# First token group's outputs stored and added in later passes, gating iterations moved into the first pass, weight sums reordered, first step in its own product order

## The chip, the cores and the metric

The kernel runs on one core of one Trainium2 chip. The metric is device time in microseconds (us). TensorE (PE) multiplies matrices into banks of the accumulation memory (PSUM); VectorE (DVE) and ScalarE (ACT) read those banks and write to on-chip memory; SyncE (SP) issues the transfers between on-chip memory and device memory, in one queue in order. Before the change the median of three runs was 1779.27 us (1777.72 to 1779.35).

## The reference

`q`, `k`, `v`, `a_re`, `a_im` have the shape (4, 8, 768, 48); `x` has 3072 tokens of 384 numbers; there are 8 experts with 1024 hidden units.

```python
for t in range(S):                                   # linear attention with a complex decay
    new_re = ar * S_re - ai * S_im
    new_im = ar * S_im + ai * S_re
    S_re, S_im = new_re + k[t] v[t]^T, new_im
    y[t] = q[t] @ S_re
x = y.transpose(0, 2, 1, 3).reshape(3072, 384)

logits = x @ w_gate                                  # 384 -> 8
P = np.exp(logits - logits.max())
for _ in range(8):                                   # the gating iterations
    P /= P.sum(1, keepdims=True) + 1e-09             # rows
    P /= P.sum(0, keepdims=True) + 1e-09             # columns
    P *= N / E
out = 0
for e in range(E):
    out += P[:, e:e + 1] * (np.maximum(x @ w1[e], 0) @ w2[e])
```

The gates P are needed only where an expert's output is added to the sum, since every expert runs on every token.

## The kernel before, in words

**Phase 1** (up to about 601 us of the profiled span) runs the attention in 12 blocks of 256 tokens and sends experts 0 and 1 along with it, block by block: `experts()` puts the first layer into `ph` (L183 to L185), the second into `po` (L162 to L164) and stores the result through `yst` to `ye_d[0]` and `ye_d[1]` in device memory. The attention's result goes as a high and a low part to `x_d`.

**Phase 2a** (L766, about 601 to 642 us) runs experts 0 and 1 for the last block. Beside it DVE and ACT build what phase 2b multiplies for the first group of 768 tokens: `load_x` (L612) loads six blocks of x (`whole`: a high part into `xt`, a low part into one of three `low` buffers, and their sum, L635), makes the sums of blocks (`form`, L645 and L647) and splits them into a high part (ACT) and a low part (`lower`, L653). `whole_w` (L745) prepares the weights of one step. `check` (L560) tests the data's range and ends with a transposition of its verdict on PE (`okp`, L573); `sinkhorn` (L577) takes the exponential; then come `HEAD` = 3 gating iterations, `rows` on DVE (L596) and `columns` (L604), whose column sum is a small matrix product with ones on PE (`cp`, L606).

**Phase 2b** (L800) runs experts 2 to 7 in 4 passes (one per group of 768 tokens) of 16 steps each, numbered n = 0 to 63. A step covers three slices of 128 hidden units of an expert and forms the first layer from 15 products instead of 18 (a fast matrix multiplication of 3x3 by 3x2 blocks): each product is a sum of weight blocks times a sum of x blocks, and takes three matmuls of 384 columns (high times high, high times low, low times high: L937, L938, L939). Two PSUM banks, A and B, are read out in turn: ACT copies the first product of a chain (L950), DVE adds or subtracts the others into `s` (L953, L972, L975), ACT applies the relu and rounds to the high part (L957), DVE takes the low part (L964). After each product come one or two of the 18 pieces of the second layer of the step before (L866 to L868), so a step is 99 matmuls. The list `slots[m]` holds side work that DVE, ACT and SP do after product m.

In the first pass (n < 16) that side work is above all the weights of step n + 1: 13 sums of weight blocks on DVE (`sums`, L714), their high parts on ACT (`hi`, L722), low parts on DVE (`lo`, L731), and stores to `w_d`, from which `fetch_w` (L764) loads them in the later passes. The raw weights come in two transfers (`raw_w`, L683). The weights of a step fill four buffers, a to d, out of a ring of `WIDE` = 11. Steps 1 to 5 of the first pass also run the last five gating iterations, with `rows` after product 6 and the column sum at the step's end; step 6 multiplies the six tiles gathered so far by their gate (L899). A finished tile of 128 tokens leaves its bank through `evict` (L832): ACT with the gate as scale for the first of the experts (L837, L839), DVE with a multiply and add for the others (L841). `mixin` (L827) adds experts 0 and 1 from `ye_d`. From step 4 or 6 on each pass also builds the x forms of the next group, one job at a time (`deal`).

What sets the order: PE's instructions run in the order of the program all through. In phase 2b DVE and ACT do so too (L1013). In phases 1 and 2a DVE and ACT, and everywhere SP, are ordered by the compiler's planner, which estimates when each instruction can run.

Of the kernel before, what the change touches and what calls it, by code (L numbers as in the profile page):

```python
# [6 lines left out]
F32 = mybir.dt.float32  # L7
F32R = mybir.dt.float32r
U8 = mybir.dt.uint8
AF = mybir.ActivationFunctionType  # L10
# [15 lines left out]
WIDE = 11  # L26
# [12 lines left out]
HEAD = 3  # L39
# [19 lines left out]
class Net:  # L59
# [9 lines left out]
    def build(self):  # L69
# [3 lines left out]
        with ExitStack() as ctx:  # L73
# [35 lines left out]
            self.ye_d = [[dram.tile([128, C], F32, name=f"ye_d{u}_{i}") for i in range(self.ntt)] for u in range(2)]  # L109
# [450 lines left out]
    def check(self, sp, more=lambda k: None):  # L560
        nc, ok, fl, ns = self.nc, self.ok, self.fl, self.N // SUB
        P = self.P.rearrange("p t e -> p (t e)")
        t = sp.tile([128, max(P.shape[1], fl.shape[1])], F32, name="chk")
        for j, (src, thr, op) in enumerate((
                (fl[:, 0:ns], 2.0 ** 40, ALU.is_le), (fl[:, ns:2 * ns], 2.0 ** 18, ALU.is_le),
                (fl[:, 2 * ns:-2], 1e-24, ALU.is_ge), (fl[:, -2:-1], 2.0 ** 40, ALU.is_le), (fl[:, -1:], 2.0 ** 18, ALU.is_le), (P, 3e38, ALU.is_le), (P, -3e38, ALU.is_ge))):
            o = t[:, :src.shape[1]]
            nc.vector.tensor_scalar(o, src, thr, None, op)
            nc.vector.tensor_reduce(ok[:, j:j + 1], o, AX.X, ALU.min)
        nc.vector.tensor_reduce(ok[:, 7:8], ok[:, 0:7], AX.X, ALU.min)  # L570
        more(2)
        tp = self.psK.tile([1, 128], F32, tag="po", name="okp")
        nc.tensor.transpose(tp, ok[:, 7:8], self.ident)  # L573
        nc.vector.tensor_reduce(ok[0:1, 8:9], tp, AX.X, ALU.min)
        nc.vector.tensor_copy(self.oki, ok[0:1, 8:9])

# [35 lines left out]
    def load_x(self, u, avail, temp, low):  # L612
# [43 lines left out]
        def plain(n, c, j):  # L656
# [9 lines left out]
            whole(*x11), whole(*x12), whole(*x21), whole(*x22),  # L666
            form(8, x11, x12, ADD), form(12, x21, 8, SUB), lower(8), form(9, x22, 12, ADD), lower(12), lower(9),
# [24 lines left out]
    def prep_w(self):  # L692
# [34 lines left out]
        def lo(q):  # L727
            t, k, src = parts[q]

            def run():  # L730
# [3 lines left out]
                if q == 3:  # L734
# [462 lines left out]
```

## Time and profile before

| | us |
|---|---|
| median of three runs | 1779.27 |
| the profiled execution | 1779.32 |
| its span | 1777.6 |
| phase 2a, in the span | 600.7 to 641.8 |
| first pass (16 steps) | 641.9 to 934.1 |
| passes 2 to 4 (48 steps) and the end | 934.1 to 1777.6 |

Some 1.7 us of the profiled execution lie around its span. In the rows of the profile `L12` is line 12 of the kernel; a group of instructions reads as count | busy us, mean ns of one | idle us of the engine just before them, and what ended it. A row of windows gives the busy time of each engine in a stretch, with the instruction count in brackets, then the share of TensorE's full clock that was granted, the share of the transfer engines and GB/s. A transfer's row ends in its size and the microseconds from issue to landing.

### The profile page before, as it was taken

What the parts mean: (1) busy time and instruction counts of PE and PEld (TensorE: products, weight loads), DVE (VectorE), ACT (ScalarE), POOL (GpSimd) and SP (SyncE); (2) the same over time, 40 slices, a digit from 0 to 9 for tenths busy, and PEclk for the clock granted to TensorE, in tenths of its full rate; (3) what the DMA queues carried; (4) which work ended last, traced back from release to release, by engine and by line L of the source; (5) the groups of instructions that cost most, each with busy time, mean ns of one, the idle gap of its engine ahead of it and who ended that gap; (6) DMA issues with size and microseconds to landing.
All of it is one profiled execution on the core that took longest, in us unless ns stands there. A gap on an engine that the chain in (4) does not pass through costs nothing.

```text
span 1777.6 us, 30741 instructions
## 1 busy us (share of the span) xinstructions
PE 1719.3 (97%) x11736; PEld 1677.5 (94%) x11736; DVE 1303.0 (73%) x2940; ACT 749.5 (42%) x1663; POOL 6.4 (0%) x15
## 2 busy tenths in 40 slices
PE   5889999999999889999999999999999999999998
PEld 3889999999999879999999999999999999999998
DVE  7888999999993669989995556655466765546564
ACT  7544554554543444544543433333433333333332
POOL 1000000000000000000000000000000000000000
PEclk9899999999999999999999999999999999999999
DMA  6333343333343657667787556667565657555560
GB/s 216 96 111 119 115 121 123 120 98 119 114 103 103 205 189 253 224 237 268 246 309 263 186 184 206 219 232 229 196 199 177 224 194 249 174 187 188 201 207 29
DMA packets 170044, 321.62 MB, mean 181 GB/s; under 512 B 13984, under 2 KB 129440, under 8 KB 169888
## 3 DMA queue, kind: packets, MB, share of 16 engines
q1 hardware_dynamic: 169088, 319.17, 54.3%
q8 instruction: 95, 1.56, 0.4%
q14 instruction: 61, 0.50, 0.1%
q10 hardware_dynamic: 800, 0.39, 0.1%
HBM read 226.64 MB, written 73.92 MB: 169 GB/s over the span
## 4 chain that ended last, share of the span: by engine, by line


## 5 line engine op out<-in xcount | busy, mean ns | idle before, releaser
L957 ACT ACTIVATE hh<-s 128x384 fp32r<-128x384 f32 x384 | 201.7, 526 | 447.1 <-DVE s L953 400.2
L953 DVE TENSOR_TENSOR s<-s,A 128x384 f32<-128x384 f32 x316 | 174.5, 552 | 141.9 <-PE A L939 140.6
L866 PE MATMUL po<-w_d,hh 128*128 128x384 f32 x768 | 257.2, 335 | 0.0
L868 PE MATMUL po<-w_d,hl 128*128 128x384 f32 x768 | 257.2, 335 | 0.0
L867 PE MATMUL po<-w_d,hh 128*128 128x384 f32 x768 | 257.2, 335 | 0.0
L964 DVE SCALAR_TENSOR_TENSOR hl<-s,hh 128x384 fp32r<-128x384 f32 x384 | 212.1, 552 | 6.9
L189 ACT ACTIVATE hh<-ph 128x256 fp32r<-128x256 f32 x192 | 73.4, 382 | 232.0 <-PE ph L185 231.4
L184 PE MATMUL ph<-xl,w 128*128 128x256 f32 x576 | 163.3, 283 | 3.4 <-DVE xl L536 3.3
L185 PE MATMUL ph<-xh,w 128*128 128x256 f32 x576 | 162.9, 283 | 0.0
L183 PE MATMUL ph<-xh,w 128*128 128x256 f32 x576 | 162.5, 282 | 0.1
L866 PEld LDWEIGHTS po<-w_d,hh 128*128 128x128 f32 x768 | 144.4, 188 | 0.5 <-DVE oa L841 0.3
L868 PEld LDWEIGHTS po<-w_d,hl 128*128 128x128 f32 x768 | 144.5, 188 | 0.0
L867 PEld LDWEIGHTS po<-w_d,hh 128*128 128x128 f32 x768 | 144.3, 188 | 0.0
L953 DVE TENSOR_TENSOR s<-s,B 128x384 f32<-128x384 f32 x192 | 106.0, 552 | 51.6 <-PE B L939 48.8
L950 ACT ACTIVATE s<-B 128x384 f32<-128x384 f32 x192 | 93.6, 487 | 109.8 <-PE B L939 107.6
L162 PE MATMUL po<-w,hh 128*128 128x384 f32 x384 | 137.4, 358 | 1.3 <-ACT yst L167 1.3
L972 DVE TENSOR_TENSOR s<-s,B 128x384 f32<-128x384 f32 x64 | 35.4, 553 | 129.7 <-PE B L939 129.5
L163 PE MATMUL po<-w,hh 128*128 128x384 f32 x384 | 130.0, 338 | 0.0
L164 PE MATMUL po<-w,hl 128*128 128x384 f32 x384 | 129.8, 338 | 0.0
L868 PE MATMUL po<-w_c,hl 128*128 128x384 f32 x384 | 128.4, 334 | 0.0
L866 PE MATMUL po<-w_c,hh 128*128 128x384 f32 x384 | 128.3, 334 | 0.0
L867 PE MATMUL po<-w_c,hh 128*128 128x384 f32 x384 | 128.3, 334 | 0.0
(235 smaller groups left out, 4079.9 us busy)
## 6 DMA issues: line engine op xcount, KB each, us to landing
w_d<-w_d SPq DMA_DIRECT2D x64, 768.0 KB, 6.3
w_a<-w_d SPq DMA_DIRECT2D x48, 768.0 KB, 7.6
w_b<-w_d SPq DMA_DIRECT2D x48, 768.0 KB, 4.2
w_c<-w_d SPq DMA_DIRECT2D x48, 768.0 KB, 4.4
raw<-in_w_dram SPq DMA_DIRECT2D x32, 576.0 KB, 5.2
w_d<-w_a SPq DMA_DIRECT2D x16, 768.0 KB, 3.2
w_d<-w_b SPq DMA_DIRECT2D x16, 768.0 KB, 4.4
w_d<-w_c SPq DMA_DIRECT2D x16, 768.0 KB, 5.9
```

What stands on the lines that cost most here:

```text
L162: nc.tensor.matmul(po[k], hh[:, s], w2h, start=f == 0, stop=False)
L163: nc.tensor.matmul(po[k], hh[:, s], w2l, start=False, stop=False)
L164: nc.tensor.matmul(po[k], hl[:, s], w2h, start=False, stop=f == NF - 1)
L183: nc.tensor.matmul(ph, w[:, 0, cs], xh[:, ct, :], start=(ct == 0), stop=False)
L184: nc.tensor.matmul(ph, w[:, 0, cs], xl[:, ct, :], start=False, stop=False)
L185: nc.tensor.matmul(ph, w[:, 1, cs], xh[:, ct, :], start=False, stop=(ct == NCT - 1))
L866: nc.tensor.matmul(po[k], hh[:, s], w2[:, 0], start=c == 0, stop=False)
L867: nc.tensor.matmul(po[k], hh[:, s], w2[:, 1], start=False, stop=False)
L868: nc.tensor.matmul(po[k], hl[:, s], w2[:, 0], start=False, stop=c == NF - 1)
L953: V.tensor_tensor(S[nm], S[nm], ps, op)
L957: A.activation(hh, S[nm], AF.Relu)
L964: V.scalar_tensor_tensor(hl, S[nm], 0.0, hh.bitcast(F32), ALU.max, ALU.subtract)
```

## The change

1. **Outputs of the first group.** In pass 1 `evict` no longer weights and adds: ACT copies each finished tile out and SP stores it to `ye_d`, which now exists for all eight experts for the first six tiles. In passes 2 to 4 each step loads one such tile (`late`) and adds it with its gate (`join`), 6 tiles by 8 experts in 48 steps. The new buffers `mo` and `my` come out of the ring of weight buffers, which shrinks from 11 to 10.
2. **Gating.** `check`, `sinkhorn` and the three iterations leave phase 2a. A generator, `gating`, does the range test, the exponential and all eight iterations in steps 1 to 14, at most six small portions per step, and asks for a PSUM bank at a step's end when it needs PE.
3. **Weights.** Phase 2a prepares the weights of steps 0 and 1, so step 0 prepares none. The sums come in another order and earlier slots, and the high and low parts in other slots (the prefix `hi(0)` moves from slot 2 to slot 3).
4. **First step.** Step 0 has no second layer to interleave. It now takes its products in the order `FIRST`, with the B chain in two banks: four products in B, copied once to `sb` and added from there, and four in F.
5. **x forms.** `load_x` loads and sums in another order; the forms for the second group are dealt from step 5 on, after products 6 and 12.

```diff
-WIDE = 11
+WIDE = 10
-WOPS = [2, 1, 7, 11, 3, 8, 12, 13, 4, 6, 14, 10, 0, 9, 5]
+WOPS = [2, 8, 6, 1, 12, 14, 3, 4, 7, 13, 10, 11, 0, 9, 5]
 PRODS = [("B", 3), ("A", 8), ("B", 12), ("A", 13), ("B", 7), ("C", 9), ("B", 1), ("C", 5), ("B", 11), ("D", 2), ("B", 10), ("E", 14), ("B", 4), ("E", 0), ("B", 6)]
+FIRST = [("B", 3), ("A", 8), ("C", 9), ("B", 12), ("A", 13), ("E", 14), ("B", 7), ("C", 5), ("B", 1), ("F", 11), ("D", 2), ("E", 0), ("F", 10), ("F", 4), ("F", 6)]
...
-            whole(*x11), whole(*x12), whole(*x21), whole(*x22),
-            form(8, x11, x12, ADD), form(12, x21, 8, SUB), lower(8), form(9, x22, 12, ADD), lower(12), lower(9),
...
+            whole(*x11), whole(*x21), form(3, x11, x21, SUB), whole(*x12), form(8, x11, x12, ADD), lower(3),
+            form(12, x21, 8, SUB), lower(8), whole(*x22), form(9, x22, 12, ADD), lower(12), lower(9),
+            whole(*x31), form(1, x12, x31, SUB), form(2, x11, x31, ADD), lower(1), lower(2), whole(*x32), form(5, x12, x32, ADD), lower(5),
...
+    def gating(self):
...
+        V.tensor_reduce(mx, flat, AX.X, ALU.max)
+        g = yield from bank([1, 128])
+        nc.tensor.transpose(g, mx, self.ident)
...
+        V.tensor_scalar(P, P, gm, None, ALU.subtract)
+        nc.scalar.activation(P, P, AF.Exp)
+        yield
+        for k in range(ITERS):
+            V.tensor_reduce(rs, P, AX.X, ALU.add)
+            yield
+            V.tensor_scalar(rs, rs, 1e-9, None, ALU.add)
+            V.reciprocal(rs, rs)
+            yield
+            V.tensor_tensor(P, P, rs.unsqueeze(2).broadcast_to([128, self.ntt, E]), ALU.mult)
+            yield
+            V.tensor_reduce(cs, P.rearrange("p t e -> p e t"), AX.X, ALU.add)
+            g = yield from bank([128, E])
+            nc.tensor.matmul(g, self.ones, cs, start=True, stop=True)
+            V.tensor_scalar(cs, g, 1e-9, None, ALU.add)
+            yield
...
-        more(1)
-        self.check(xa, more)
-        self.sinkhorn(xa, more)
-        for k in range(HEAD):
-            self.rows()
-            more(3)
-            self.columns(self.psK.tile([128, E], F32, tag="po", name=f"cp{k}"))
-            if k == 1:
-                self.raw_w(0)
-                self.raw_w(1)
-                self.whole_w()
+        for _ in range(2):
+            self.raw_w(0)
+            self.raw_w(1)
+            self.whole_w()
...
+        def late(m, q):
+            tt = tile_of(0, m)
+            t = home[q] = self.xa.tile([128, C], F32, tag="my" if q else "mo", name=f"m{q}_{tt}", bufs=2)
+            nc.sync.dma_start(t, self.ye_d[q][tt])
+
+        def join(m, q):
...
+                V.scalar_tensor_tensor(o, home[q], self.P[:, tt, q:q + 1], o, ALU.mult, ALU.add)
...
         def evict(u, e, k):
+            if u == 0:
+                st = self.xa.tile([128, C], F32, tag=f"oa{k}", name=f"st{e}_{tt}")
+                A.activation(st, po[k], AF.Copy)
+                nc.sync.dma_start(self.ye_d[e][tt], st)
+                return
...
-            if n + 1 < NT:
+            if 1 <= n and n + 1 < NT:
                 slots[1] += [sums(0, 3)]
-                slots[2] += [sums(3, 6), hi(0)]
-                slots[3] += [sums(6, 10)]
-                slots[4] += [sums(10, 12), hi(1)]
-                slots[5] += [sums(12, 13), lo(0), hi(2), hi(3)]
-                slots[6] += [lo(1), hi(4)]
+                slots[2] += [sums(3, 8)]
+                slots[3] += [sums(8, 13), hi(0)]
+                slots[4] += [hi(1)]
+                slots[5] += [hi(2), hi(3), lo(0)]
+                slots[6] += [hi(4), lo(1)]
...
-            if n in sink:
-                slots[6].append(self.rows)
+            if 1 <= n:
+                for m in (2, 4, 7, 8, 10, 12):
+                    slots[m].append(lambda: next(gate, None))
...
+            if u:
+                d, q = 2 * (u - 1) + t // E, t % E
+                slots[6].append(lambda: join(d, q))
+                if n + 1 < len(steps):
+                    slots[7].append(lambda: late(d + (q == E - 1), (q + 1) % E))
...
+                def whole_b(ps):
+                    sb = S["sb"] = xt.tile([128, TH], F32, tag="xt0", name="sb")
+                    A.activation(sb, ps, AF.Copy)
+                    s31(ps)
+                    add("s11", sb, SUB)
+                    add("s12", sb)
+                    add("s22", sb)
+                    s21(sb)
...
-            if n in sink:
-                self.columns(self.psA.tile([128, E], F32, tag="ph", name=f"cp{n}"))
+            if self.want:
+                g = self.psA.tile(self.want, F32, tag="ph", name=f"g{n}")
                 flips[0] += 1
+                self.want = None
+                gate.send(g)
```

**Where instructions move, 1: ACT in step 1.** `s_1_...` are the copies of products out of the banks, `w_a`, `w_b` and `w_c` the high parts of step 2's weights, made of the sums on DVE. Before:

```order
L950 ACTIVATE s_1_8885<-B_8881 128x384
L950 ACTIVATE s_1_8899<-A_8880 128x384
L722 ACTIVATE w_a<-sum_8879 128x768
L950 ACTIVATE s_1_8912<-B_8881 128x384
L722 ACTIVATE w_b<-sum_8879 128x768
L950 ACTIVATE s_1_8935<-B_8881 128x384
```

and with the change:

```order
L1015 ACTIVATE s_1_8861<-B_8857 128x384
L1015 ACTIVATE s_1_8875<-A_8856 128x384
L1015 ACTIVATE s_1_8891<-B_8857 128x384
L702 ACTIVATE w_a<-sum_8855 128x768
L702 ACTIVATE w_b<-sum_8855 128x768
L1015 ACTIVATE s_1_8915<-B_8857 128x384
```

The copy of the third product no longer stands behind a weight conversion; the copy of the fifth stands behind two.

**2: DVE, the gating beside a step's readouts.** `rs`, `cs`, `P` are the gating's row sums, column sums and gates. Before, in step 1:

```order
L731 TENSOR_TENSOR w_b<-sum_8879,w_b 128x768
L598 TENSOR_REDUCE rs<-P 128x24
L599 TENSOR_SCALAR rs<-rs 128x24
L600 RECIPROCAL rs<-rs 128x24
L601 TENSOR_TENSOR P<-P,rs 128x192
L602 TENSOR_REDUCE cs<-P 128x8
L972 TENSOR_TENSOR s_1_8967<-s_1_8899,B_8881 128x384
```

and with the change, in step 3, its first iteration:

```order
L787 TENSOR_REDUCE rs<-P 128x24
L711 TENSOR_TENSOR w_a<-sum_9246,w_a 128x768
L711 TENSOR_TENSOR w_b<-sum_9246,w_b 128x768
L1037 TENSOR_TENSOR s_3_9339<-s_3_9265,B_9248 128x384
L711 TENSOR_TENSOR w_c<-sum_9246,w_c 128x128
L711 TENSOR_TENSOR w_c<-raw_4_9143,w_c 128x256
L789 TENSOR_SCALAR rs<-rs 128x24
L790 RECIPROCAL rs<-rs 128x24
L1018 TENSOR_TENSOR s_3_9306<-s_3_9306,A_9247 128x384
L711 TENSOR_TENSOR w_c<-raw_4_9209,w_c 128x384
L792 TENSOR_TENSOR P<-P,rs 128x192
```

One block of five operations ahead of the product's readout has become portions between readouts.

**3: SP, the x loads of phase 2a.** `X` are plain operands, loaded as they are; `xt` are parts that DVE sums. Before, the last of them:

```order
L624 DMA X_0_8259<-x_d_94 128x3x128 x2
L624 DMA X_0_8262<-x_d_94 128x3x128 x2
L624 DMA xt_0_8205<-x_d_94 128x3x128
L624 DMA xt_0_8210<-x_d_94 128x3x128
L168 DMA ye_d_20_142<-yst_10_0_8268 128x384
```

and with the change:

```order
L607 DMA X_0_8295<-x_d_94 128x3x128
L607 DMA xt_0_8235<-x_d_94 128x3x128
L607 DMA X_0_8295<-x_d_94 128x3x128
L607 DMA X_0_8298<-x_d_94 128x3x128 x2
L867 DMA m_0_11934<-ye_d_0_98 128x384
L867 DMA m_0_11999<-ye_d_0_122 128x384
L867 DMA m_2_13188<-ye_d_2_100 128x384
L607 DMA xt_0_8246<-x_d_94 128x3x128
L168 DMA ye_d_20_142<-yst_10_0_8384 128x384
L607 DMA xt_0_8261<-x_d_94 128x3x128
```

The two last parts of x stand one behind other transfers: three loads for the later passes and a store that waits for ACT have come ahead of the last of them.

More of the change, by code (lines that the diff above doesn't have):

```diff
@@ L558, in logits @@
         yield
[L560 to L575, printed above, removed]
     def sinkhorn(self, sp, more=lambda k: None):
@@ L811, in phase2b @@
         avail = [(xc, f"xc{k}") for k in range(4)]
-        sink = range(1, 1 + ITERS - HEAD)
+        home = {}
+        gate = self.gating()
         def acc(e, u, k):
@@ L977, in step @@
             reads = {
-                1: lambda ps: copy("s11", ps),
-                2: lambda ps: copy("s21", ps),
-                3: lambda ps: copy("s12", ps, -1.0),
-                4: lambda ps: add("s11", ps, SUB),
-                5: lambda ps: copy("s32", ps, -1.0),
-                6: lambda ps: copy("s22", ps, -1.0),
-                7: s31,
-                8: lambda ps: (add("s32", ps), high(2, 1, "s32")),
-                9: lambda ps: (add("s11", ps, SUB), high(0, 0, "s11")),
-                10: lambda ps: (add("s31", ps), high(2, 0, "s31")),
@@ L988, in step @@
-                11: lambda ps: add("s12", ps),
-                12: lambda ps: add("s22", ps, SUB),
-                13: lambda ps: (add("s22", ps), high(1, 1, "s22")),
-                14: lambda ps: (add("s12", ps, SUB), high(0, 1, "s12")),
-                15: lambda ps: (s21(ps), high(1, 0, "s21")),
-            }
+                3: lambda ps: copy("s11", ps),
+                8: lambda ps: copy("s21", ps),
+                12: lambda ps: copy("s12", ps, -1.0),
+                13: lambda ps: add("s11", ps, SUB),
@@ new lines, in step @@
+                7: lambda ps: copy("s32", ps, -1.0),
+                9: lambda ps: copy("s22", ps, -1.0),
+                1: s31,
+                5: lambda ps: (add("s32", ps), high(2, 1, "s32")),
+                11: lambda ps: (add("s11", ps, SUB), high(0, 0, "s11")),
+                2: lambda ps: (add("s31", ps), high(2, 0, "s31")),
+                10: lambda ps: add("s12", ps),
+                14: lambda ps: add("s22", ps, SUB),
+                4: lambda ps: (add("s22", ps), high(1, 1, "s22")),
@@ new lines, in step @@
+                0: lambda ps: (add("s12", ps, SUB), high(0, 1, "s12")),
+                6: lambda ps: (s21(ps), high(1, 0, "s21")),
+            }
+            lowers.append(low(1, 0, "s21"))
+            if n == 0:
+                def whole_b(ps):
[6 more added lines that the diff above has]
+                    s21(sb)
+                reads[1] = whole_b
+                reads[0] = lambda ps: add("s12", ps, SUB)
+                reads[10] = lambda ps: (add("s12", ps), high(0, 1, "s12"))
+                reads[6] = lambda ps: (add("s21", ps, SUB), high(1, 0, "s21"))
+                after = {11: low(2, 1, "s32"), 0: low(0, 0, "s11"), 10: low(2, 0, "s31"), 4: low(0, 1, "s12"), 6: low(1, 1, "s22")}
+                for c, k in FIRST:
+                    reads[k](prod(c, k))
+                    if k in after:
+                        after[k]()
+                return
@@ L998, in step @@
             slots[15].insert(0, low(0, 1, "s12"))
-            lowers.append(low(1, 0, "s21"))
             for m, (c, k) in enumerate(PRODS, 1):
-                reads[m](prod(c, k))
+                reads[k](prod(c, k))
                 for g in slots[m]:
```

97 lines of the change are left out of this document (70 added, 27 removed).

## The prediction

> **What bounds the kernel now.** I read the page's shares first, then a table of windows by stage, then the list of waits, then the timeline at the long waits.
>
> ```profile
> span 1777.6 us, 30741 instructions
> PE 1719.3 (97%) x11736; PEld 1677.5 (94%) x11736; DVE 1303.0 (73%) x2940; ACT 749.5 (42%) x1663; POOL 6.4 (0%) x15
> ...
> 600.70:641.80 41.10, 35.57 (x225) 34.44 (x224) 28.67 (x85) 19.63 (x49) 0.00 (x0) 0.92 0.38 135
> 641.80:655.10 13.30, 10.14 (x48) 7.43 (x47) 10.30 (x22) 8.33 (x18) 0.00 (x0) 1.00 0.75 251
> 655.10:676.40 21.30, 17.89 (x102) 17.17 (x100) 17.68 (x43) 9.26 (x19) 0.00 (x0) 1.00 0.87 323
> 676.40:748.90 72.50, 72.12 (x408) 69.34 (x406) 68.53 (x177) 36.91 (x75) 0.00 (x0) 1.00 0.67 238
> 748.90:917.00 168.10, 161.50 (x893) 155.37 (x894) 157.09 (x369) 81.43 (x164) 0.00 (x0) 0.99 0.72 251
> 917.00:934.10 17.10, 17.10 (x100) 17.10 (x99) 15.47 (x32) 8.72 (x19) 0.00 (x0) 1.00 1.02 349
> 934.10:1768.00 833.90, 833.69 (x4789) 829.24 (x4788) 493.96 (x955) 288.44 (x569) 0.00 (x0) 1.00 0.59 198
> ```
>
> The windows' columns are the stretch and its length, busy time and count of PE, weight load, DVE, ACT, POOL, then clock, transfer share, GB/s. PE is the bound: 97% busy, and 833.69 of 833.90 us in passes 2 to 4, where nothing can be gained without fewer matmuls; the change removes none there. An undisturbed step is the one of 917.0 to 934.1, 17.1 us. What can be won lies in phase 2a (row 1) and the first pass, 641.9 to 934.1 = 292.2 us. Its 15 steps after step 0 would take 15 x 17.1 = 256.5; they take 292.2 - 13.3 = 278.9, so 22.4 us are lost there: 21.3 - 17.1 = 4.2 in step 1, 72.5 - 4 x 17.1 = 4.1 in steps 2 to 5, 168.1 - 9 x 17.1 = 14.2 in steps 6 to 14. There DVE is 17.68 of 21.3, 68.53 of 72.5, 157.09 of 168.1 us busy: it is nearly the second bound. In passes 2 to 4 it has 41% free.
>
> ```profile
> PE B L937 <- ACT s L950: 9.0, 9, 3.3
> PE okp L573 <- DVE ok L570: 3.9, 1, 3.9
> PE po L162 <- ACT yst L167: 1.3, 1, 1.3
> PE cp L606 <- DVE cs L602: 0.3, 1, 0.3
> ...
> 606.45:609.86 3.41, 0.52 (x5) 0.31 (x3) 3.41 (x8) 1.70 (x5) 0.00 (x0) 1.00 0.56 231
> 609.86:613.27 3.41, 2.36 (x9) 2.40 (x10) 3.02 (x10) 1.08 (x3) 0.00 (x0) 0.50 0.56 233
> 613.27:616.69 3.42, 3.42 (x15) 3.33 (x15) 1.97 (x5) 1.65 (x5) 0.00 (x0) 0.50 0.62 150
> ```
>
> The waits (total us, times, longest) say what the losses are; the three windows say that the transposition of the check's verdict, 3.9 us late, also costs clock: a window with 0.52 us of PE work is followed by two at half clock.
>
> **Part 1, phase 2a: about -8.** The check, the exponential and three iterations go. With them go the wait for `ok` 3.9, the half clock (2.36 + 3.42 us of work at 0.5 is 2.9 lost), the wait for `cs` 0.3, the wait for `yst` 1.3 (it stood behind form conversions on ACT, whose order is new), and PE's own gating work, a transposition and three column sums:
>
> ```profile
> L606 PE MATMUL cp<-cs,ones 128*128 128x8 f32 x16 | 2.4, 220 | 0.3 <-DVE cs L602 0.3
> 610.91 0.37 PE L573 MATMUL okp<-ident,ok 128*1 128x128 f32 x1 [3.94 <-DVE ok L570]
> ```
>
> 0.37 + 3 x 0.22 = 1.0. Sum 9.4. Against it stands the longer load of x. SP issues one part in 5.27 / 8 = 0.66 us, and the last low part was issued in 595.56 to 597.55 with its sum on DVE from 599.50, 3.9 us after the row's start:
>
> ```profile
> 590.19 5.27 SPq L624 DMA_DIRECT2D X<-x_d  x8
> 595.56 1.99 SPq L624 DMA_DIRECT2D xt<-x_d  x2
> 599.50 1.12 DVE L635 TENSOR_TENSOR xt<-xt,xt 128x384 f32<-128x384 f32 x2 [3.10 <-DMA xt<-x_d]
> ```
>
> In the new order the low ring's three buffers also hold forms between the loads, and the last low part stands behind three loads and a store that waits for ACT. I put its issue at 601.7 (estimate: the part before it at about 597, then that part's flight and two or three operations of DVE at 1.12 / 2 = 0.56), its landing 3.9 later, and with six more DVE operations the low part of the experts' fourth unit at 608.4, where PE wants it at about 607.05: 1.3 us of stall. From below it is 0 (DVE passes the experts' part first); from above 4, as long as the check's wait, with its half clock. I take 1.3: gain 8.1. One weight preparation comes from step 0 into phase 2a, where DVE had 41.1 - 28.67 = 12.4 us free and loses the gating's work.
>
> **Part 2, step 0: +1.4.** It has 45 matmuls, 15 x 3, against 99, and is paced by readouts.
>
> ```profile
> 642.57 0.49 ACT L950 ACTIVATE s<-B 128x384 f32<-128x384 f32 x1
> 644.53 0.56 DVE L953 TENSOR_TENSOR s<-s,A 128x384 f32<-128x384 f32 x1 [4.44 <-PE A L939]
> ```
>
> A product takes 17.1 / 33 = 0.52 of PE, a copy 0.49, a DVE readout 0.56. In the new order four products run into B without a readout, but the copy to `sb` comes after the ninth product and five DVE operations hang on it (s31, then s11, s12, s22, s21), before F's first readout; F's next three products then wait for one another's. Played through with these durations, the step takes 13.1 us: no gain. The waits, though, bunch: PE idle about 2.0, 1.7 and 0.8 us within 6 us, where before they were spread over the step. What bunching does to the clock:
>
> ```profile
> 657.65:661.06 3.41, 1.79 (x11) 1.47 (x9) 1.10 (x5) 0.08 (x1) 0.00 (x0) 1.00 1.05 416
> 753.22:756.63 3.41, 1.57 (x9) 1.31 (x8) 3.31 (x11) 3.17 (x7) 0.00 (x0) 1.00 0.00 0
> 756.63:760.04 3.41, 3.41 (x13) 3.41 (x12) 0.91 (x2) 1.51 (x5) 0.00 (x0) 0.50 0.76 317
> ```
>
> The window with 1.79 us of PE work was followed by full clock (the row of step 1 has 1.00 for all of it), the one with 1.57 by half. Two waits of 2.0 and 1.7 with the work between leave well under 1.57 in most positions of such a window. The next window at half clock loses 1.7 us, or two 3.4; where it falls well, none. I take 1.4 (0 to 3.4). The Trainium skill, "TensorE: Matmul & The Clock Gate", section "Why this matters for your kernels", puts the limit at PE-idle gaps of more than about 3 us; by it this term would be 0. Its section "Part 1: The HAM clock gate (the "warmup" mystery)" has the free-running window of about 3.4 us, with which these rows agree, but here work of 1.57 us in a window did not keep the clock.
>
> **Part 3, steps 1 to 15: about -15.** Where the 22.4 us are now:
>
> ```profile
> 662.75 0.44 PE L937 MATMUL B<-X,w_a 128*128 128x384 f32 x1 [3.30 <-ACT s L950]
> 652.32 1.74 SPq L683 DMA_DIRECT2D raw<-in_w_dram  x1
> DVE sum L714 <- DMA raw<-in_w_dram: 7.8, 3, 2.7
> 748.90:770.90 22.00, 19.97 (x101) 18.60 (x102) 18.66 (x47) 11.14 (x23) 0.00 (x0) 0.92 0.55 202
> L899 ACT ACTIVATE oa<-oa,P 128x384 f32<-128x384 f32 x6 | 3.2, 604 | 0.0
> ```
>
> Step 1's 3.30: a copy on ACT stands behind a weight conversion, that behind DVE's sums, these behind raw weights issued at 652.32. In the change raw weights two steps ahead are asked for in phase 2a and step 0 prepares nothing, so they lie ready: 3.3 goes. Step 6's 22.0 - 17.1 = 4.9: six scalings of 0.604 on ACT in its first slots, then the half clock shown above. `evict` no longer needs P, so there are none: 4.9 goes. The rest, 14.2, is DVE's work in lumps: the gating block,
>
> ```profile
> 683.58 0.34 DVE L598 TENSOR_REDUCE rs<-P 128x24 f32<-128x192 f32 x1
> ...
> 685.34 0.54 DVE L972 TENSOR_TENSOR s<-s,B 128x384 f32<-128x384 f32 x1
> L841 DVE SCALAR_TENSOR_TENSOR oa<-po,P,oa 128x384 f32<-128x384 f32 x120 | 71.6, 612 | 27.5 <-PE po L868 27.5
> L830 DVE SCALAR_TENSOR_TENSOR oa<-y,P,oa 128x384 f32<-128x384 f32 x48 | 29.4, 612 | 0.0
> L837 ACT ACTIVATE oa<-po 128x384 f32<-128x384 f32 x6 | 2.8, 486 | 0.5 <-PE po L868 0.5
> L592 ACT ACT_TABLE_LOAD x1 | 1.3, 1283 | 0.0
> ```
>
> 1.76 us (683.58 to 685.34) ahead of one readout, and evictions and `mixin`s at 0.612. Thirty evictions and twelve `mixin`s leave DVE in the first pass, 42 x 0.612 = 25.7 us; ACT takes 30 copies more at 0.486, on an engine that is half idle there. The gating comes in portions of 0.3 to 0.6 us. What stays of loss: eleven banks for it, 0.22 and a switch of banks, 0.25 each (estimate), 2.8; the exponential with its table load, 1.28, ahead of a copy in step 3, 1.0; 0.5 in each of five steps where x jobs fill DVE; a DVE that in step 1 first takes all thirteen sums, 0.285 each by the row
>
> ```profile
> L714 DVE TENSOR_TENSOR sum<-raw 128x128 f32<-128x128 f32 x80 | 20.0, 285 | 7.8 <-DMA raw<-in_w_dram 7.8
> ```
>
> ahead of the fourth product's readout, 0.9 later than now, with the weights' low parts behind it: 1.1 in all. Sum 7.4, so the 15 steps take 263.9 and 15.0 are won. Bounds: 2 stay (gain 20) and 19 stay, as a lump of 1.1 in each (gain 3).
>
> **Part 4, passes 2 to 4: +1.** A `join` is 0.61 on DVE, 42 of them in 833.9 us where DVE has 340 free, and six on ACT at 0.60: hidden, unless one delays a readout; 0 to 4, taken as 1. With ten weight buffers a load starts when an earlier buffer of the ring is given back, for the last of a step's four about 2 us later than now by the order of the products.
>
> ```profile
> 1226.70 0.32 SPq L764 DMA_DIRECT2D w_d<-w_d  x1
> w_d<-w_d SPq DMA_DIRECT2D x64, 768.0 KB, 6.3
> ```
>
> This one is for step 34, which begins at 934.1 + 18 x 17.1 = 1242 or later; by the median it lands at 1226.70 + 6.3 = 1233.0, 9 us ahead. With 2 less, 7 remain: nothing. SP issues 36 stores of tiles, 48 loads and 6 stores more, 0.3 each by this row, over 1000 us.
>
> **Sum.** -8.1 + 1.4 - 15.0 + 1.0 = -20.7. The profiled execution, span 1777.6 and 1.7 around it, took 1779.32, the median 1779.27: 1758.6, say **1758.5**. About 0.2% (3.6 us) is what a measurement of this kernel can tell from no change.
>
> **Rivals.**
> *All smooth:* no half clock after step 0 (-1.4), no stall in phase 2a (-1.3), 5 us of the 7.4 not lost: about 1751. For it: DVE has the room; against: step 0's waits follow from the durations.
> *The skill's gap rule alone:* 1.4 less, 1757.2, too near the forecast to be told by the time, but by the clock in the window after step 0. Against it stands the row at 753.22.
> *DVE stays the second bound:* the preparing steps still take 16 to 17.7 us of DVE. With a stall of 0.8 more in each of 14 steps, 11 more: 1770. For it: DVE 157.09 of 168.1 now; against: 25.7 us have left.
> *The load of x stalls phase 2a as the check did:* 3.9 + 2.9 in place of 1.3: 1764.
> *Slower: the column sum arrives late.* Its last operand moves from slot 6 to slot 12, three products before PE asks for it at the step's end. If DVE is more than the 3.6 us late that lie between (three products with their pieces), PE waits at eleven step ends; at 2.2 us each, with a window at half clock (1.7), 43 us against the 20.7: 1801. For it: the engine is in order and full; against: its queue behind slot 8 holds readouts alone, and these pace PE already.
> *That it does nothing* is excluded as far as the rows of phase 2a go: `ok` and three column sums leave PE's order.
>
> **How the numbers follow.** Forecast 0.44, the skill's rule 0.12, smooth 0.18, DVE bound 0.16, x loads 0.05, slower 0.05. The range takes smooth to 1747 and the DVE case to 1771: outside lie the slower case, and about a third of the two outer ones. Faster holds all but the slower case, less 0.02 for a DVE case so deep that nothing is left: 0.93, 0.02, 0.05.
>
> **What would show it.** In phase 2a: no half clock, phase 2b beginning about 633.7. Step 0 some 13 us with two waits near 2 us, and half a clock after it. Step 1 under 19 us, no wait over 1 us on `s` there. Step 6 about as its neighbours. The first pass about 278.6 us; passes 2 to 4 as long as now, to 1 us. Column sums without waits. It is wrong if phase 2b begins after 637, or if steps 2 to 14 average over 18.3.

## The result and the profile after

The changed kernel takes 1754.24 us (median of four runs, 1753.96 to 1757.18) against 1779.31 before; the ratio is 0.9863, 95% interval 0.9846 to 0.988. The forecast was 1758.5, the range 1747 to 1771, so the median lies 4.3 under the forecast. The execution with the profile is the slowest of the four, 1757.18, 1.3 under the forecast and 22.1 under the profiled execution of before, 1779.32. The stages below are those of that one execution.

The page of the changed kernel, its shares, and a table of windows by stage (step 0, step 1, step 2, steps 3 to 5, steps 6 to 15, passes 2 to 4). The columns are the stretch and its length, busy time and count of PE, weight load, DVE, ACT and POOL, then clock, transfer share and GB/s:

```profile
span 1755.4 us, 30926 instructions
PE 1711.6 (98%) x11736; PEld 1678.9 (96%) x11736; DVE 1294.7 (74%) x2944; ACT 762.8 (43%) x1694; POOL 6.4 (0%) x15
...
634.51:648.57 14.06, 9.65 (x47) 8.19 (x47) 8.34 (x17) 6.12 (x13) 0.00 (x0) 0.91 0.48 146
648.57:667.78 19.21, 19.21 (x102) 19.12 (x101) 16.05 (x42) 8.74 (x18) 0.00 (x0) 0.89 0.47 169
667.78:685.43 17.65, 17.65 (x104) 17.39 (x102) 14.92 (x37) 9.11 (x18) 0.00 (x0) 1.00 0.71 255
685.43:738.32 52.89, 52.86 (x305) 52.19 (x304) 48.49 (x132) 29.59 (x60) 0.00 (x0) 1.00 0.77 273
738.32:912.38 174.06, 174.06 (x1002) 173.30 (x1003) 160.00 (x420) 98.20 (x200) 0.00 (x0) 1.00 0.83 290
912.40:1746.20 833.80, 833.62 (x4788) 829.16 (x4787) 513.38 (x991) 293.99 (x581) 0.00 (x0) 1.00 0.57 210
```

From step 2 on PE is busy all through: 52.86 of 52.89, 174.06 of 174.06. Passes 2 to 4 take the same 833.8 us as before with 19 us more of DVE in them (513.38 against 493.96), so the 48 joins are hidden. The first pass takes 912.4 - 634.5 = 277.9 us, before 292.3: 14.4 less. What is left of loss is in steps 0 and 1, where the clock stands at 0.91 and 0.89. Around those, windows of 3.41 us:

```profile
639.26:642.67 3.41, 1.98 (x12) 1.66 (x10) 2.44 (x6) 0.90 (x2) 0.00 (x0) 1.00 0.77 221
642.67:646.08 3.41, 1.13 (x5) 0.81 (x6) 3.41 (x8) 1.41 (x3) 0.00 (x0) 1.00 0.73 208
646.08:649.50 3.42, 2.77 (x9) 2.27 (x8) 1.79 (x5) 0.80 (x3) 0.00 (x0) 0.50 0.01 3
649.50:652.91 3.41, 3.41 (x12) 3.41 (x12) 3.29 (x15) 1.30 (x3) 0.00 (x0) 0.50 0.00 0
...
643.41 0.44 PE L1002 MATMUL F<-X,w_b 128*128 128x384 f32 x1 [2.17 <-DVE s L1018]
645.74 0.44 PE L1002 MATMUL F<-X,w_b 128*128 128x384 f32 x1 [1.54 <-DVE s L1018]
```

PE waits 2.17 and 1.54 us for DVE's readouts of bank F, a window gets 1.13 us of PE work, and the next two run at half clock.

The starts of the spans differ. From the start of the same matmul of phase 1 (the 531st of the 576 in the third line of the experts' first layer) to phase 2b the two kernels take, before and after:

```profile
594.97:641.85 46.88, 41.35 (x266) 39.94 (x265) 31.19 (x91) 21.75 (x57) 0.00 (x0) 0.93 0.43 146
596.15:634.51 38.36, 37.67 (x257) 35.87 (x256) 25.91 (x62) 22.07 (x60) 0.00 (x0) 1.00 0.84 308
```

8.5 us are won there, and the half clock is gone; the matmul itself starts 1.2 us later. Of the 22.2 us between the spans, 8.5 come from phase 2a, 14.4 from the first pass, 0.4 from what follows it, and phase 1 takes 1.2 back.

### The profile page after: what moved, and what is told of

Same layout as the page of the kernel before. It is cut to its first block, busy times and chain, and to the rows that moved or that the text cites. A ratio compares the mean times of both kernels' runs of the same rounds, so it can differ in the third digit from the quotient of the medians.

```text
span 1755.4 us, 30926 instructions
## 1 busy us (share of the span) xinstructions
PE 1711.6 (98%) x11736; PEld 1678.9 (96%) x11736; DVE 1294.7 (74%) x2944; ACT 762.8 (43%) x1694; POOL 6.4 (0%) x15
## 4 chain that ended last, share of the span: by engine, by line
```

## The experiments

In all of them phase 1 and passes 2 to 4 issue what the changed kernel issues, except in the one built on the kernel before and in the two with copies on DVE, whose last six copies fall in step 16. That same matmul of phase 1 starts between 592.2 and 596.7 us in the profiles, so the runs' times scatter by some us; from the same matmul on, the stages that an edit leaves alone repeat to some tenths where the clock is the same. The first four runs after the change's own ran side by side on one chip, and their medians can be compared. For the others, which ran beside a kernel before that itself went from 1774.67 to 1786.54, a difference of a few us between medians says little: by the intervals of the ratios, only the outputs alone and the copies with mixing stand apart from the changed kernel. What is read from them below is read from the stages of one profile each. "2a" is the time from that matmul to phase 2b, "first pass" from the first matmul of step 0 to that of step 16.

| run | median | before beside it | ratio, interval | 2a | first pass |
|---|---|---|---|---|---|
| before | 1779.27 | | | 46.9 | 292.3 |
| the change | 1754.24 | 1779.31 | 0.9863 (0.9846 to 0.988) | 38.4 | 277.9 |
| again | 1756.76 | 1779.22 | 0.9875 (0.9859 to 0.989) | 39.1 | 278.4 |
| step 0 in the old order | 1752.55 | 1779.22 | 0.9846 (0.9833 to 0.986) | 39.0 | 272.9 |
| waits filled | 1753.58 | 1779.22 | 0.9851 (0.9837 to 0.9865) | 39.0 | 275.1 |
| DVE's order in step 0 | 1755.71 | 1779.22 | 0.9866 (0.9851 to 0.9881) | 38.8 | 276.2 |
| gating's head in 2a | 1762.13 | 1781.62 | 0.9887 (0.9857 to 0.9917) | 49.3 | 274.4 |
| copies on DVE | 1760.36 | 1781.62 | 0.9875 (0.9843 to 0.9907) | 39.1 | 281.5 |
| copies and mixing on DVE | 1767.94 | 1781.37 | 0.9926 (0.9905 to 0.9948) | 38.6 | 288.1 |
| old order of the sums | 1759.25 | 1781.62 | 0.9874 (0.9842 to 0.9905) | 38.7 | 280.7 |
| gating in blocks | 1762.53 | 1781.62 | 0.9885 (0.9855 to 0.9915) | 39.1 | 283.7 |
| old order, weights in step 0 | 1757.50 | 1779.24 | 0.9877 (0.9844 to 0.991) | 38.8 | 280.3 |
| old order, old x loads | 1752.14 | 1779.24 | 0.9847 (0.9814 to 0.9879) | 38.8 | 272.7 |
| outputs alone, on the kernel before | 1769.04 | 1779.24 | 0.9935 (0.9915 to 0.9956) | 45.8 | 283.0 |

### The changed kernel again

> The changed kernel itself, again, as the measure for the three runs beside it. Its four times so far were 1753.96 to 1754.27 and once, with the profile, 1757.18. If the 3 us between them are the half clock after step 0 (two windows of 3.4 us at half clock, 3.4 us of work lost), the time goes by steps of about 1.7 us from run to run, as the windows happen to fall: 1754 to 1757. If they are jitter of transfers in phase 1, it varies without steps.

The four times are 1756.14 to 1758.52. In this profile the window of step 0 holds 1.27 us of PE work, and three windows run at half clock, not two; step 0 and 1 together take 33.8 us against 33.3. The clock moves the time, then, but by half a microsecond here; phase 1 moves it more (the matmul above starts at 592.8 here, at 596.15 in the first profile). The steps of 1.7 that were expected cannot be seen in so few times.

### Step 0: its order, the clock, DVE

Undone, the first step's own order:

```diff
-            if n == 0:
-                def whole_b(ps):
...
-                for c, k in FIRST:
-                    reads[k](prod(c, k))
...
             for m, (c, k) in enumerate(PRODS, 1):
                 reads[k](prod(c, k))
```

> Undoes the first step's own order alone: step 0 takes the products in the order of the other steps, with eight products one after the other in bank B, each read before the next. Theory (step 0's waits are DVE's four additions of sb, and step 0 prepares no weights any more): a B product waits only 0.2 to 0.3 us for its readout, seven times, so step 0 takes 7.8 + 7 x 0.27 = 9.7 to 10.5 us in place of 14.1, no window falls under 1.57 us of PE work, the clock stays at 1.00 and step 1 takes 17.4 to 18.0 in place of 19.2. Some of it comes back since DVE is then behind in step 1: 2 to 5 us faster than the changed kernel. Rival (the order is what makes up for the missing work: with B's chain in one bank the step takes 13.2 us as before the change): the same as the changed kernel or up to 1 us faster.

Steps 0 and 1 and the rest of the first pass:

```profile
634.92:645.96 11.04, 9.86 (x46) 7.33 (x46) 6.00 (x12) 5.22 (x11) 0.00 (x0) 1.00 0.61 184
645.96:663.30 17.34, 17.34 (x101) 17.05 (x101) 16.43 (x44) 9.34 (x19) 0.00 (x0) 1.00 0.53 191
663.30:907.81 244.51, 244.48 (x1407) 242.76 (x1406) 223.32 (x588) 136.93 (x276) 0.00 (x0) 1.00 0.81 284
```

The theory holds: 11.0 and 17.3 us in place of 14.3 and 19.5 beside it, clock 1.00, 5.5 us less in the first pass and 4.2 in the median of the runs beside it. Only step 0 is half a microsecond over its 9.7 to 10.5. The new order of step 0 is a loss inside the change: without weights to prepare, the products in one bank wait 0.6 us at most, and the four additions of `sb` are extra work for DVE just ahead of F's first readout. Whether the new order would pay in a step 0 that also prepares weights, no run shows.

Filling the waits with matmuls that nobody reads:

```diff
+                idle = {10: 12, 4: 9, 6: 4}
                 for c, k in FIRST:
+                    for _ in range(idle.get(k, 0)):
+                        nc.tensor.matmul(dm, W[3][0][:, 0, W[3][1]], X[3][:, 0], start=True, stop=True, skip_group_check=True)
                     reads[k](prod(c, k))
```

> The changed kernel with 25 more matmuls in step 0 that nobody reads, put into its three waits (12, 9 and 4, at 0.17 us each). Nothing else moves. Theory (a window with little PE work halves the clock): clock 1.00 after step 0, step 0 as long as before or 0.5 shorter, step 1 17.4 to 17.8 us in place of 19.2; every run at the fast end, 1754 or 1 to 2 below it. Rival (the gap rule of the Trainium skill's TensorE page: a gap under 3 us does not matter, the half clock in the profile came from elsewhere): half clock at the same place all the same, no change in time.

```profile
635.60:648.90 13.30, 13.18 (x71) 11.99 (x71) 8.34 (x17) 6.13 (x13) 0.00 (x0) 1.00 0.51 153
648.90:666.09 17.19, 17.19 (x101) 17.10 (x101) 15.95 (x42) 8.73 (x18) 0.00 (x0) 1.00 0.53 189
```

Nothing else is changed, 25 matmuls are added, and the clock stays at 1.00: step 1 takes 17.2, the first pass 3.4 us less, the median 3.2 less than the changed kernel's beside it. So it was the idle time of PE that halved the clock, and waits of 2.2 us at most do it.

The third run leaves the products' order and lets DVE read F before three of its additions; it also puts the readout of bank D and the low parts behind later products:

```diff
                     s31(ps)
                     add("s11", sb, SUB)
-                    add("s12", sb)
-                    add("s22", sb)
-                    s21(sb)
...
+                reads[0] = lambda ps: (add("s12", S["sb"]), add("s12", ps, SUB))
```

> The changed kernel's products in its order, but DVE adds sb to s12, s22 and s21 only when those sums are due, after it has read F for the first time. Theory (PE waits in step 0 for DVE's block of additions): the first wait of 2.3 becomes 0.9, the second 1.7 becomes 0.8, step 0 takes 11 us in place of 14.1 and the clock stays; in step 1 up to 1.7 us come back since DVE's low parts are still to do: 1 to 4 us faster than the changed kernel. Rival (DVE is the bound of steps 0 and 1 together, whatever the order): step 0 shorter, step 1 longer by as much, the same time within 1 us.

```profile
633.54:645.77 12.23, 9.59 (x46) 8.13 (x46) 7.21 (x14) 6.09 (x13) 0.00 (x0) 0.91 0.52 159
645.77:665.03 19.26, 19.26 (x101) 19.17 (x101) 17.35 (x45) 8.75 (x18) 0.00 (x0) 0.88 0.51 179
...
640.04:643.45 3.41, 1.48 (x7) 0.90 (x6) 3.10 (x8) 0.97 (x2) 0.00 (x0) 1.00 0.93 267
643.45:646.87 3.42, 2.77 (x10) 2.27 (x9) 2.80 (x6) 1.34 (x4) 0.00 (x0) 0.50 0.12 35
```

Half right. Step 0 is 2.1 shorter and step 1 as long as before, so DVE's order was a cause and the time is not given back. But the clock falls all the same: the waits are now 0.93, 1.00 and 0.65 us, and one window with two of them still holds only 1.48 us of work.

### Phase 2a: the gating's head back

```diff
+        more(1)
+        self.check(xa, more)
+        self.sinkhorn(xa, more)
+        for k in range(HEAD):
+            self.rows()
+            more(3)
+            self.columns(self.psK.tile([128, E], F32, tag="po", name=f"cp{k}"))
...
-        for k in range(ITERS):
+        for k in range(ITERS - HEAD):
```

> The changed kernel with the range test, the exponential and the first three gating iterations back in phase 2a, as before the change; the other five in the first pass. Theory (the prediction's part 1): PE waits for the verdict some 3 to 4 us there, with two windows at half clock behind, and phase 2b begins 7 to 9 us later; the first pass is as long or 1 us shorter: 6 to 9 us slower than the changed kernel. Rival (the wait of before came from the x loads' order, and the new order leaves DVE room): 0 to 3 slower.

Phase 2a of this kernel (the row begins one matmul, 0.1 us, early), its steps 2 to 15, and PE's longest wait in phase 2a; then steps 2 to 15 of the changed kernel in its second profile:

```profile
594.01:643.42 49.41, 40.99 (x267) 39.75 (x266) 35.11 (x101) 24.87 (x63) 0.00 (x0) 0.93 0.68 242
676.20:917.80 241.60, 241.60 (x1397) 241.23 (x1396) 216.69 (x540) 135.22 (x274) 0.00 (x0) 1.00 0.82 288
PE cp L607 <- DVE cs L603: 5.7, 1, 5.7
```

```profile
665.70:910.40 244.70, 244.67 (x1408) 242.95 (x1407) 223.50 (x588) 137.00 (x276) 0.00 (x0) 1.00 0.81 284
```

Phase 2a is 10.2 us longer than in the changed kernel (39.1), the clock falls again, and steps 2 to 15 are 3.1 shorter; with steps 0 and 1, which lost less to the clock this time, the first pass is 4.0 shorter than there (278.4). Net 6.2, in the theory's 6 to 9, but only as a sum: phase 2a was to grow by 7 to 9 and the first pass to shrink by 1 at most. The wait has moved: the verdict is 0.5 us late, a column sum 5.7. Between the exponential and that column sum, 617 to 624 us, DVE's rows are mostly sums and low parts of the second step's weights. So PE waits in phase 2a for a gating result that stands between DVE's preparations, and in the first pass the same work costs 3.1 us. Since this kernel prepares two steps' weights in phase 2a, it does not repeat the waits of before one by one.

### DVE's work in the first pass

Thirty tile copies from ACT to DVE, 24 of them in the first pass and six in step 16; then also two multiply-and-adds in each of steps 8 to 13:

```diff
-                A.activation(st, po[k], AF.Copy)
+                if e > 2:
+                    V.tensor_copy(st, po[k])
+                else:
+                    A.activation(st, po[k], AF.Copy)
```

> The changed kernel with 30 of the first pass's 36 tile copies (experts 3 to 7) on DVE instead of ACT, a plain copy at about 0.55 us: 16.5 us of DVE's work in steps 4 to 16. Theory (DVE is the second bound of the first pass, and its evictions made the losses of 1.6 to 2.4 in steps 9, 11, 12 and 14): 3 to 8 us slower than the changed kernel, in the steps with six evictions. Rival (those losses came from the multiplications of experts 0 and 1 and the x forms; DVE now has room): under 1 us slower.

```diff
+            if not u and 8 <= t < 8 + 2 * NS:
+                def mix():
+                    y, z = self.xa.tile([128, C], F32, tag="y0", name=f"mx{n}"), X[3][:, 0].bitcast(F32)
+                    V.scalar_tensor_tensor(y, z, self.P[:, t, 0:1], z, ALU.mult, ALU.add)
+                for q in range(2):
+                    slots[13 + q].append(mix)
```

> The run with 30 copies on DVE, and besides two multiply-and-adds of 0.6 us on DVE in each of steps 8 to 13 after products 13 and 14, where experts 0 and 1 were mixed in before the change (they write a tile nobody reads). With the copies alone the first pass lost 2.0 in step 6, 1.3 in step 8 and 0.5 in step 9, and nothing in steps 11, 12 and 14. Theory (the losses of before in steps 9, 11 and 12 were evictions and mixing together, DVE's total per step being the bound): 0.5 to 1.5 us more in each of steps 8 to 13, 4 to 8 us over the run with the copies alone. Rival (those losses were the x forms' places, after products 9 and 14): under 1.5 us over it, steps 9 and 12 under 18 us.

Steps 6, 7, 8 and 9 to 15 with the copies alone, then steps 6, 8 and 9 of the second kernel:

```profile
734.60:754.10 19.50, 18.76 (x101) 17.28 (x101) 19.39 (x53) 9.24 (x19) 0.00 (x0) 1.00 0.82 289
754.10:771.70 17.60, 17.58 (x102) 17.50 (x102) 16.93 (x47) 9.19 (x19) 0.00 (x0) 1.00 0.73 253
771.70:790.60 18.90, 18.13 (x102) 17.36 (x102) 18.76 (x51) 9.19 (x19) 0.00 (x0) 1.00 0.80 271
790.60:912.80 122.20, 122.04 (x699) 120.67 (x700) 114.80 (x296) 61.55 (x122) 0.00 (x0) 1.00 0.83 289
```

```profile
738.10:757.60 19.50, 18.73 (x102) 17.25 (x102) 19.38 (x53) 9.25 (x19) 0.00 (x0) 1.00 0.83 290
775.10:795.10 20.00, 18.44 (x103) 17.34 (x102) 19.86 (x53) 9.21 (x19) 0.00 (x0) 1.00 0.80 270
795.10:815.20 20.10, 19.08 (x101) 18.80 (x101) 18.71 (x51) 9.13 (x18) 0.00 (x0) 0.92 0.67 238
```

The copies cost 4.0 us in steps 2 to 15 (664.1 to 912.8 = 248.7 against 244.7; over the whole first pass 3.0, since steps 0 and 1 lost less to the clock this time), the lower half of the theory, and nearly all of it in steps 6 and 8, where six of them meet the gating and DVE is busy 19.39 of 19.5 us; in steps 11 and 14, with six copies but little or no gating, they cost under 0.3. With the mixing the first pass is 6.7 longer still, spread over steps 8 to 13. That is in the theory's 4 to 8, but some 1.7 of it is one window at half clock in step 9 (0.92 in its row). In these runs a step loses time where DVE's total fills it, not by a single operation. Of the losses of before, this brings back that of step 9: 20.2 us, 18.5 without the half clock, against 18.0 with the copies alone and 19.6 before. Step 12 takes 17.5 and step 14 17.3, where the kernel before took 18.8 in both, so there the copies and the mixing are not enough. The rival's places for the x forms, after products 9 and 14, are not enough alone either: the run with the outputs alone, below, keeps them and takes 17.2 in both steps. The two together were not tested.

### The sums' order and the gating in blocks

```diff
-                slots[2] += [sums(3, 8)]
-                slots[3] += [sums(8, 13), hi(0)]
-                slots[4] += [hi(1)]
+                slots[2] += [sums(3, 6), hi(0)]
+                slots[3] += [sums(6, 10)]
+                slots[4] += [sums(10, 12), hi(1)]
...
```

> The changed kernel with the old order of the weight sums and the old places of sums, high and low parts in the step. Theory (the weights' reordering only keeps the third product's copy from standing behind a conversion, and removes 0 to 0.6 us a step where DVE is late): 1 to 6 us slower, in waits on ACT's copies. Rival (with evictions and lumps gone DVE is in time anyway): the same within 1 us.

```diff
             V.tensor_reduce(rs, P, AX.X, ALU.add)
-            yield
             V.tensor_scalar(rs, rs, 1e-9, None, ALU.add)
             V.reciprocal(rs, rs)
-            yield
             V.tensor_tensor(P, P, rs.unsqueeze(2).broadcast_to([128, self.ntt, E]), ALU.mult)
-            yield
```

> The changed kernel with the row part of each gating iteration as one block of five operations (1.8 us of DVE) in place of portions. Theory (the prediction's part 3: the block cost 0.5 to 0.8 us in each of steps 2 to 5): 0.3 to 0.8 in each of eight steps, 2 to 6 us slower. Rival (the loss of steps 2 to 5 was the column sum's bank, and DVE's lateness in a step is caught up before PE asks): the same within 1 us.

Steps 2 to 15 with the old order of the sums; with the gating in blocks, and PE's wait of that kernel:

```profile
663.90:911.90 248.00, 245.68 (x1407) 241.89 (x1406) 228.64 (x588) 135.27 (x276) 0.00 (x0) 1.00 0.79 278
```

```profile
666.00:917.00 251.00, 245.50 (x1408) 241.98 (x1407) 227.49 (x588) 137.02 (x276) 0.00 (x0) 1.00 0.78 276
PE A L999 <- DVE s L1015: 5.5, 7, 0.8
```

Against 244.7 the old order costs 3.3 us: 0.5 in step 3 and about 0.4 in each of steps 5 to 11. The size fits its theory, the place only in part: PE waits once for a copy on ACT (0.8 us) and five times for a readout on DVE (0.3 each). The blocks cost 6.3: 0.9 to 1.1 more in each of the seven steps 4 to 10, with a wait of 0.8 for one readout that stands behind the block. That theory holds in kind and is a little short in size (0.3 to 0.8 a step, 6 in all).

### Weights two steps ahead, x loads, outputs alone

The first kernel has the old order of step 0 and prepares step 1's weights in step 0 again:

```diff
-        for _ in range(2):
-            self.raw_w(0)
-            self.raw_w(1)
-            self.whole_w()
+        self.raw_w(0)
+        self.raw_w(1)
+        self.whole_w()
...
-            if 1 <= n and n + 1 < NT:
+            if n + 1 < NT:
```

> The changed kernel with the first step's old order and with the weights of step 1 prepared in step 0 again, instead of in phase 2a; to be read against the run with the old order alone (step 0 11.0 us, step 1 17.3, phase 2a 39.0 from the same matmul). Theory (the prediction's part 3: step 1's wait came from raw weights asked for too late, and step 0 is lengthened by the preparation): step 0 13 us, step 1 20 to 21 with a wait of 2 to 3.5 on a copy or on DVE's sums, phase 2a the same or up to 1 shorter: 4 to 6 us slower than the old order alone. Rival (the new places of the sums and the x loads' order do it without the earlier preparation): step 1 under 18.5, 2 us slower in all.

```profile
633.15:645.08 11.93, 9.90 (x47) 7.33 (x46) 8.90 (x17) 8.11 (x17) 0.00 (x0) 1.00 0.68 242
645.08:668.90 23.82, 20.45 (x101) 19.71 (x101) 17.33 (x45) 9.46 (x19) 0.00 (x0) 0.86 0.76 281
PE A L1000 <- DVE s L1016: 2.9, 1, 2.9
```

The first pass takes 7.4 us more than with the old order alone (280.3 against 272.9), above the expected 4 to 6, and the median 5.4 more than that of the next run, which is beside it and as long as the old order alone in these stages. The wait of step 1 is back at 2.9 us, and this time the clock falls with it. In the trace the raw weights are issued at 644.24 and 646.66, DVE waits 3.4 us for them, and the readout that PE waits for stands behind the sums made of them. So it is the raw weights that lie ready, not the places of the sums, that remove the wait, and the preparation ahead is the larger part of what steps 0 and 1 give.

The second has the old order of step 0 and `load_x` as before the change:

> The changed kernel with the first step's old order and the old order of the x loads and sums. Theory (the prediction's part 1: the new load order costs phase 2a a stall, here 0.7 on a low part of the experts): phase 2a 0.5 to 1 us shorter than with the old step order alone, steps 0 to 15 the same. Rival (the new load order does nothing, or gives step 0 its operands earlier): phase 2a the same within 0.3, or step 0 longer.

Phase 2a takes 38.75 against 38.98 and the first pass 272.7 against 272.9. The rival holds: the load order makes no difference that could be told. 1752.14 is the fastest median of all; between it and 1752.55 nothing can be told, and both kernels are 5 us shorter than the changed one in the first pass.

The third is the kernel before with the outputs of the first group stored and joined later, and nothing else:

> The kernel before with part 1 of the change alone: the first group's tiles copied out on ACT and stored, added up in later passes, ring of ten weight buffers; gating, weights, step 0 and x forms as before. Theory (the prediction's part 3): step 6's 4.9 us go, and most of the 8 us in steps 9, 11, 12 and 14; steps 1 to 5 keep theirs (7.5 us), phase 2a keeps its waits, passes 2 to 4 stay as they are: 9 to 12 us faster than before. Rival (DVE's room is taken by the rest, the parts help only together): step 6 alone improves, 4 to 5 us faster.

Steps 0 and 1, 2 to 5, 6, and 7 to 15:

```profile
641.04:677.80 36.76, 30.40 (x147) 27.31 (x146) 28.27 (x64) 17.55 (x36) 0.00 (x0) 0.91 0.78 277
677.80:750.20 72.40, 72.07 (x407) 69.31 (x406) 68.44 (x177) 36.86 (x75) 0.00 (x0) 1.00 0.72 258
750.20:768.50 18.30, 17.84 (x102) 17.20 (x101) 16.11 (x41) 10.70 (x23) 0.00 (x0) 1.00 0.82 294
768.50:924.00 155.50, 155.50 (x894) 154.37 (x892) 140.59 (x324) 86.58 (x177) 0.00 (x0) 1.00 0.81 287
```

Step 6 goes from 22.0 to 18.3, steps 7 to 15 from 163.2 (770.9 to 934.1) to 155.5, steps 2 to 5 stay. 11.5 us are won from step 6 on, and steps 0 and 1 lose 2.2 of them, since the clock now falls with the wait of step 1 that before the change it survived: 9.3 in the first pass, 10.2 in the median, inside the expected 9 to 12. Of the parts that were tested this is the largest, though the others were measured by taking them out of the change and this one by putting it into the kernel before.

## Why the prediction held, point by point

- **The sum** was -20.7 in the profiled execution's terms; measured -22.1, after phase 1, where PE's work was not changed, had taken 1.2 back. The median fell by 25.1, and when the changed kernel ran again by 22.5. The profiled execution is the slowest of its four, so that it fits the forecast to 1.3 us is in part luck. By the time alone the median of 1754.24 lies as near to the smooth rival's 1751 as to the forecast; the half clock after step 0, which that rival excludes, is what speaks for the forecast.
- **Phase 2a, -8.1:** -8.5 from the same matmul on; phase 2b began at 634.5, 633.7 was forecast. The stall by the longer x loads, put at 1.3, was mis-sized: the wait on that low part is 0.5 in the list of waits, and the run with the old loads gains 0.2. That gating results make PE wait and cost the clock in phase 2a is shown by the run with the head back, though there the wait sits on a column sum and not on the verdict; what each of the four waits of before was worth was not measured one by one.
- **Step 0, +1.4:** right in the mechanism and short in size. 14.06 us against 13.1 worked out; the waits 2.17 and 1.54 where 2.0 and 1.7 were expected; the half clock came in all eight profiles of kernels with the new order and without filler. Against the run with fillers it costs 0.8 in step 0 (14.06 against 13.30) and 2.0 in step 1 (19.21 against 17.19), 2.8 where 1.4 was taken, inside the 0 to 3.4. The comparison it rested on was incomplete: "no gain" was measured against a step 0 that still prepared weights. Against the old order without that work the new one loses 5.5 us.
- **The Trainium skill's gap rule** ("TensorE: Matmul & The Clock Gate", section "Why this matters for your kernels"), given 0.12, does not hold here as the prediction read it, that a shorter gap leaves the clock alone. The measurement decides: with waits of 2.2 us at most, and in one run of 1.0 at most, the clock was halved.
- **Steps 1 to 15, -15.0:** 912.4 - 648.6 = 263.8 us, 263.9 were forecast, but errors cancel, and the agreement to 0.1 is luck. Of the 7.4 of remaining loss, 1.1 in step 1 did not come (17.2 to 17.3 with the clock held), nor the 2.5 for the x forms as a loss of its own; steps with a gating bank take 17.4 to 17.65, 0.2 to 0.5 over an undisturbed one where 0.25 was taken. Step 3's exponential is 0.8 over an undisturbed step, not 1.0. In their place stands the 2.0 of the clock, which had been booked under step 0. The 25.7 us that were to leave DVE were counted too high: of the thirty evictions six fall in step 16, and those of the first pass are 24, with the twelve `mixin`s 21.6 us. The sum does not use that number, only the argument against the rival that DVE stays the second bound.
- **What the 15 us were made of** was right: the outputs' part (11.5 from step 6 on when alone), the raw weights (7.4 in steps 0 and 1, half clock included), portions in place of blocks (6.3), the sums' order (3.3). Together they are more than 15 and cannot be added: the first is what it wins alone, the others what is lost when one of them is taken out; that they share DVE's time is the likely reason, and no run shows it. One reading was too simple: evictions alone did not make the losses of before. With the mixing part of step 9's comes back; what made those of steps 12 and 14 together with them is open, but they go when the outputs are stored (17.2 each with the outputs alone).
- **Passes 2 to 4, +1.0:** 833.80 against 833.90, nothing. Ten weight buffers are enough.
- **The other rivals:** the slower one did not come about, as no column sum is waited for in the changed kernel. Steps 2 to 14 average 17.5 us, so DVE does not stay the second bound to the extent of 18.3, and phase 2b began at 634.5, so the load of x did not stall phase 2a as the check did.

## What to carry to other kernels

When work is moved out of a stage, plan that stage again from what is left in it: once step 0's weight preparation was gone, its old order was 5.5 us faster than the new one. Where a second engine is nearly as full as the first, cut its queue into portions no longer than the slack before the next result that the first one waits for, and count its total per step: either alone is not enough. Short waits close together should be judged by how much work is left in a clock window, not one by one.

## What the runs showed of the hardware

The clock follows the work in windows of 3.41 us, not the length of a wait. A stretch at half clock lasts one such window (756.63 to 760.04 before), two (646.08 to 652.91 after) or more, and the rows here are cut at that grid. Windows that were followed by half clock hold 0.52, 1.57 (before), 1.13 (after), 1.27, 1.48, 1.02 and 1.44 us of PE work (the repeat, DVE's order, outputs alone, weights in step 0); ones that were not hold 1.79 and, right behind it, 1.72 (before) and 1.98 (after) or more. One window does not fit a single border: in step 8 of the run with copies and mixing 1.86 us were followed by half clock. The window of 1.72 and that one, with the one behind it:

```profile
661.06:664.47 3.41, 1.72 (x10) 1.72 (x11) 3.27 (x11) 2.17 (x4) 0.00 (x0) 1.00 0.70 273
792.22:795.64 3.42, 1.86 (x11) 1.45 (x10) 3.42 (x8) 1.05 (x2) 0.00 (x0) 1.00 0.80 243
795.64:799.05 3.41, 3.41 (x13) 3.25 (x12) 3.38 (x16) 0.98 (x2) 0.00 (x0) 0.50 0.93 336
```

So in these windows 1.57 us of work or less lost the clock, 1.98 or more kept it, and in between it went either way. Of the 1.86 us, 0.39 are a column sum of 8 columns; whether such small matmuls count for less is not shown.

A wait of 3.3 us in step 1 left the clock alone in the kernel before, where it fell over two windows (1.79 and 1.72), and the same step with a wait of 3.2 lost it with the outputs alone, where one window held the most of it:

```profile
657.62:661.03 3.41, 1.02 (x6) 0.69 (x5) 1.92 (x8) 0.47 (x1) 0.00 (x0) 1.00 1.04 426
661.03:664.44 3.41, 2.60 (x8) 2.61 (x9) 3.34 (x9) 2.48 (x6) 0.00 (x0) 0.50 0.55 211
```

That the position of the wait in the window makes this difference is read from these two profiles; no run shifted the one against the other. The 25 useless matmuls that held the clock are worth 2.8 to 3.4 us in the first pass (275.1 against 277.9 and 278.4), and they only fill waits.
